# Attention and gated MLP on one core: the two output banks of a burst copied side by side into one buffer and stored with five transfers, and the loads of a stack issued in one block

## The chip, the core and the metric

The kernel runs on one NeuronCore of a Trainium2 chip. The metric is the device time of one execution in microseconds (us). A comparison is made of medians of several runs on the same chip.

## What is computed

With x of 2048 tokens by 512 features, the reference is

```python
g = sigmoid((x * gate_w).sum(-1, keepdims=True))
q, k, v = x @ wqkv                      # 32 heads of 16, sliding window of 256 keys, causal
a = softmax(mask(q k^T * 16**-0.5)) v @ wo
b = (sigmoid(x @ w_gate) * (x @ w_up)) @ w_down     # hidden width 1376
out = g * a + (1 - g) * b
```

Inputs and output are float32. The kernel splits each operand into a high and a low part and adds three products for each matmul.

## The kernel before

Tokens are handled in 16 blocks of 128 and 4 chunks of 512. The 32 heads form 8 groups of four. A *step* is one group with one chunk (32 steps), and two steps share one slot of `ring`, a buffer with three slots in which queries and keys of eight blocks stand stacked in rows: a high part, a low part, a row of zeros or ones, and a row that takes the negated maximum of each query.

The main loop (line 839) runs over *units* u, one unit per group and block, and a unit holds four heads. In unit u TensorE computes the scores of block u (`s_part`, L370), from which VectorE takes the row maxima (L376), and the transposed scores of block u - 9 (`st_part`, L425), of which ScalarE takes exponentials (L430) into `pbuf` or `pwide`. Between these matmuls stand the products of the projections (`pj`) and of the gate and up weights (`gu`), both L282. PE's order, like those of VectorE, ScalarE and SyncE (SP), is the order in which the program writes it (`manual_schedule`), and each engine works through its instructions in that order.

The maxima take a way through memory. Every fourth unit (`mark`) `max_split` (L383) makes the high and low part of the negated maxima of a step, `max_store` (L394) writes them to `max_scratch`, and `max_load` (L401, two transfers) reads them back into the ring's maximum row. `st_part` needs that row for the query blocks j to j + 2 of the same group. In units 29, 45, 61 and so on the loaded maxima are those of the third chunk of a group, and `st_part` asks for them two units later, in units 31, 47, 63. In units 21, 37 and so on they are those of the first chunk of a new group, which `st_part` asks for in the unit after the next burst.

Every eighth unit from 17 to 121 (14 units, `visits[u] == 2`) has a *burst*: `pv_part` (L460) multiplies the exponentials of two steps with v, first into the bank `pv` and then into a second bank. `o_take` (L468) copies a bank on ScalarE into a buffer `ob` (one of five buffers with the tag `sp`, which also serve the results of `gu` and `pj`) and leaves five transfers in the list `later`: four of 16 rows for the heads' outputs (`oT_d`) and one for the sums (`sum_d`). `run_dmas` (L342) issues a list on SP. In the same burst the two halves of the next stack are split (`proj_hi`, `proj_lo`) and written to `stack_scratch`.

Behind the burst, in the units with u % 8 == 2, `stack_load` (L317) makes the list `sdma` of six transfers (in the first stacks seven) that fill the next ring slot: one of constants and five from `stack_scratch`. The function `transfers` (line 859) issues what stands in `later` and then the first `SD` = 3 entries of `sdma`, so that a stack's loads are spread over two units with what is in `later` between them. The stack is used by `s_part` from the unit u % 8 == 0 that follows.

`pbuf` has 15 slots of 128 x 512. In the groups before the last the exponentials use slots 0 to 11 of it; in the last group all 15.

Of the kernel before, what the change touches and what calls it, by code (L numbers as in the profile page):

```python
# [19 lines left out]
DH = 16  # L20
HG = 4
NG = H // HG
CH = 512
NC = T // CH
# [16 lines left out]
PVLAG = LAG + 4  # L41
WIDE = 2 * 4
NWIDE = NG - 1
SD = 3
QB = 32
HOLD = 3
GAPS = [3] * 12 + [2] * 3
# [18 lines left out]
def gated_mix_kernel(  # L66
# [77 lines left out]
    with ExitStack() as actx:  # L144
# [323 lines left out]
        def o_take(s, bank):  # L468
# [5 lines left out]
                later.append((oT_d[h * DH:(h + 1) * DH, c * CH:(c + 1) * CH], ob[32 * hh:32 * hh + DH]))  # L474
            later.append((sum_d[c, g * HG:(g + 1) * HG], ob.rearrange("(h r) f -> r h f", r=32)[DH]))

        def proj(s):
            for k in range(3 * ND):
                proj_mm(s, k)
            proj_hi(s)  # L480
            proj_lo(s)
# [357 lines left out]
        for u in range(N):  # L839
            if u == LAG:  # L840
                vctx.close()
                pctx = ExitStack()
                ppool = pctx.enter_context(tc.tile_pool(name="ppool", bufs=1))
                pbuf = ppool.tile([P, 15, HG, P], F32, name="pbuf")
                pv = ps.tile([P, CH], F32, tag="pv", name="pv", bufs=1)
            if u == 1:
                proj_post(NC)
            if u == 4:
                load_gu(0, 0)
                load_gu(0, 1)  # L850
            if (u == LAG or u % 8 == 2 and u > 10) and u // 8 + 1 < NP:
                sdma = stack_load(u // 8 + 1)
            if u % 16 == 8 and u // 16 + 2 < NG:
                raw_q = load_wqk(u // 16 + 2)
            if u in (4, 8, NU):
                max_store(u // 4 - 1)
            mark = PVLAG <= u < NU and (u - PVLAG) % 4 == 0

            def transfers():
                if mark and visits.get(u) != 2:  # L860
                    run_dmas(later[:2])
                    del later[:2]
                    max_load((u - 5) // 4)
                run_dmas(later)
                later.clear()
                run_dmas(sdma[:SD])
                del sdma[:SD]

            if u in V_STORE:
                v_store(V_STORE[u])  # L870
            if not mark:
                transfers()
            if u in (5, LAG):
                max_load(u // 4 - 1)
            if u in V_LOAD:
                v_load(V_LOAD[u])
            if u in WD_LOAD:
                load_d(WD_LOAD[u])
            if u == NU:
                max_load(NSTEP - 1)  # L880
            if u in TAIL_LOAD:
                tail_load(TAIL_LOAD[u])
            if u == WO:
                both = apool.tile([P, ND, CH], F32, tag="w0", name="woraw")
                wo_raw.extend(both[:, d] for d in range(ND))
                nc.sync.dma_start(both, wo.rearrange("(c p) n -> p c n", p=P))
            for s4 in proj_at.get(u, ()):
                if u < LAG:
                    first.insert(0, (
                        lambda k, h, s4=s4: proj_slot(s4, k, h), lambda s4=s4: proj_sum(s4)))  # L890
                else:
                    work.append(proj_group(s4))
            if u == N - 1:
                hold_group(*rest.pop(0))
            for hh in range(HG):
                wide = visits.get(u) == 2
                if hh == 0 and u in visits:
                    s2 = (u - PVLAG) // 4 - wide
                    pv_part(s2, pv)
                if hh == 3 and mid(u + 1):  # L900
                    max_split((u - 4) // 4)
                if hh == 0 and mark:
                    if not mid(u):
                        max_split((u - 5) // 4)
                    run_dmas(later)
                    later.clear()
                    max_store((u - 5) // 4)
                if hh == 0 and wide:
                    flush(evac)
                    ripe = [held.pop(0) for _ in range(2) if held and held[0] // 2 == u // 8 + 1]  # L910
                    for s4 in ripe:
                        proj_hi(s4)
                    o_take(s2, pv)
                    run_dmas(later)
                    later.clear()
                    max_load((u - 5) // 4)
                    for s4 in ripe:
                        proj_lo(s4)
                    run_dmas(later)
                    later.clear()  # L920
                    second = ps.tile([P, CH], F32, tag="st", name=f"pv{s2}", bufs=2)
                    pv_part(s2 + 1, second)
                    for guests, n in ((acts, 2), (behind, 3)):
                        for _ in range(min(n, len(guests))):
                            guests.pop(0)()
                    o_take(s2 + 1, second)
                elif hh == 0 and u in visits:
                    evac.append(lambda s2=s2: o_take(s2, pv))
                if hh == 2 and mark:
                    transfers()  # L930
                if u < NU:
                    s_part(u, hh)
                if 0 <= u - LAG < NU:
                    st_part(u - LAG, hh ^ 1 if u < NU else hh)
                if u < LAG:
                    flush(behind)
                    if hh % 2 == 1:
                        upto = n_first * (2 * u + 1 + hh // 2) // (2 * LAG)
                        run_first(upto - done)
                        done = upto  # L940
                else:
                    long = u < U_WIDE
                    k8 = (u - LAG) % WIDE * HG + hh
                    dense = GAPS2[max(0, k8 - 1)] < 3 if long else u < NU and (u - PVLAG) % 4 == 3 and hh > 0
                    k = (u - PVLAG) % 4 * HG + hh
                    free = hh == 2 and not mid(u + 1) if long else k in (1, 5, 9) or k in (3, 7) and len(behind) > 2
                    if behind and (u < PVLAG or u >= NU or free):
                        behind.pop(0)()
                    if evac:
                        evac.pop(0)()  # L950
                    elif acts and not dense and (u < NU or hh % 2 == 1):
                        acts.pop(0)()
                if u >= LAG and (hh % 2 == 1 or u < NU) and (u + 1 not in visits or hh < HG - 1):
                    if u < N - 2:
                        next(slots)
            if u < LAG:
                flush(soon)
            if u == LAG - 1:
                split_gu(0, 0)
                split_gu(0, 1)  # L960
            if u in (3, 7, NU - 1):
                max_split(u // 4)
            if u // 16 + 2 < NG:
                if u % 16 == 10:
                    acts.append(lambda g=u // 16 + 2, r=raw_q: (
                        split_wqk(g, r, 0), behind.insert(0, lambda: split_wqk(g, r, 1))))
            if 0 <= u - LAG < NU:
                mask_p(u - LAG)
            if u in TAIL_SPLIT:
                acts.append(lambda d=TAIL_SPLIT[u]: tail_split(d))  # L970
            if u in WD_SPLIT:
                acts.append(lambda f=WD_SPLIT[u]: split_d(f, True))
            if u in WO_SPLIT:
                acts.extend(lambda d=d: wo_split(d) for d in range(WO_SPLIT[u], WO_SPLIT[u] + 1))
            if u in SUMS:
                sums_load(SUMS[u])
            if u - 2 in SUMS:
                behind.append(lambda c=SUMS[u - 2]: later.append(sums_invert(c)))
            if u == TREAD:
                tail_reads(0)  # L980
            if u >= TREAD:
                tail_read(0, 2)
            for n in H_LOAD.get(u, ()):
                h_load(n)
            if u == N - 1:
                pctx.close()
                lpool = actx.enter_context(tc.tile_pool(name="lpool", bufs=1))
                gates = lpool.tile([P, 4 * NB], F32, name="gates")
                gs, omg = gates[:, 0:NB], gates[:, NB:2 * NB]
                spare = [lpool.tile([P, CH], F32, name=f"spare{k}") for k in range(6)]  # L990
            if u >= N - 2:
                flush(evac)
                flush(acts)
                flush(behind)
                h_skew(u - N - 1)
# [164 lines left out]
```

## Time and profile before

| | us |
|---|---|
| median of 3 runs | 729.6 (725.34 to 729.9) |
| the profiled execution, as a run | 723.27 |
| its span, first to last instruction | 721.4 |
| PE busy | 713.5 |
| VectorE, ScalarE, GpSimd busy | 478.5, 430.4, 165.6 |
| bytes moved by DMA | 127.22 MB, 176 GB/s over the span |

The granted TensorE clock of the span is 1.000. The 14 bursts begin at 94.14, 123.88, 155.44, 184.97, 215.85, 245.22, 275.70, 305.27, 337.22, 366.59, 397.53, 426.99, 459.10 and 488.85 us: the starts of the pieces "PE pv L460" in the chain of waits. So a burst with its number of units can be found in the trace: unit 17 is at 94.14, unit 25 at 123.88, and so on in steps of eight. SPq is the queue of SyncE, whose instructions are the DMA issues; the duration of such a row is the time that the issue holds the queue, and not the time of the transfer. In a table of stretches each row gives for a stretch its length, each engine's busy time with the number of instructions, the granted clock, the mean busy share of the 16 DMA engines, and GB/s.

### The profile page before, as it was taken

How to read it: one execution, taken by the hardware profiler on the slowest of the kernel's cores; microseconds unless marked ns; L12 is line 12 of the kernel's file. 1: busy time of each engine (PE TensorE's matmuls, PEld its weight loads, DVE VectorE, ACT ScalarE, POOL GpSimd, SP SyncE). 2: the span in 40 equal slices, each digit the busy share in tenths (PEclk: the TensorE clock that was granted, in tenths of full speed). 3: DMA queues.
4: the chain of work that ended last, by engine and by line, in shares of the span. 5: the costliest groups of instructions: out<-in, count | busy, mean ns of one | idle time of the engine just before them, and what ended most of it. 6: DMA issues, size and time to landing. Idle time of an engine off the chain costs nothing.

```text
span 721.4 us, 17549 instructions
## 1 busy us (share of the span) xinstructions
PE 713.5 (99%) x6298; PEld 606.1 (84%) x6298; DVE 478.5 (66%) x1455; ACT 430.4 (60%) x890; POOL 165.6 (23%) x254
## 2 busy tenths in 40 slices
PE   9999999999999999999999999999999999999997
PEld 7888889888798798988979889798788888888886
DVE  5369767657676676765667667676837767667481
ACT  6423766667676677766767667675676655435341
POOL 5200423223233233323324223232331000000000
PEclk9999999999999999999999999999999999999999
DMA  8465534646355364554645437465478978778531
GB/s 304 112 201 195 202 123 177 189 137 212 127 195 189 121 211 146 178 165 146 203 149 197 152 99 245 151 219 148 154 216 227 263 201 215 199 169 250 144 65 58
DMA packets 104814, 127.22 MB, mean 176 GB/s; under 512 B 46718, under 2 KB 63614, under 8 KB 104728
## 3 DMA queue, kind: packets, MB, share of 16 engines
q1 hardware_dynamic: 104584, 125.98, 56.2%
q8 instruction: 49, 0.80, 0.5%
q14 instruction: 37, 0.30, 0.1%
q10 hardware_dynamic: 144, 0.13, 0.1%
HBM read 71.80 MB, written 51.13 MB: 170 GB/s over the span
## 4 chain that ended last, share of the span: by engine, by line
PE 98%; DMA 1%; issue 0%; DVE 0%; DVEq 0%
PE gu L282 28%; PE pj L282 12%; PE pv L460 11%; PE s L370 6%; PE st L425 6%; PE tp L598 6%; PE pd L96 5%; PE pd L95 5%; PE pd L94 5%; PE vh L635 3%; PE pa L94 2%; PE pa L95 2%; PE pa L96 2%; PE vps L497 2%; DMA ring<-max_scratch 1%; PE pd L1088 1%
## 5 line engine op out<-in xcount | busy, mean ns | idle before, releaser
L376 DVE CUSTOM_DVE_ANT_0 junk<-s,mask 128x384 f32<-128x384 f32 (+2 forms) x512 | 271.9, 531 | 136.8 <-PE s L370 76.4
L282 PE MATMUL gu<-xh,w 64*128 64x512 f32 x1152 | 273.5, 392 | 0.0
L282 PE MATMUL gu<-xl,w 64*128 64x512 f32 x576 | 185.9, 389 | 0.0
L430 ACT ACTIVATE pbuf<-st 128x384 f32<-128x384 f32 (+2 forms) x288 | 138.3, 490 | 60.7 <-PE st L425 31.3
L425 PE MATMUL st<-ring 64*128 64x384 f32 (+2 forms) x536 | 166.6, 327 | 2.7 <-DMA ring<-max_scratch 2.5
L370 PE MATMUL s<-ring 64*128 64x384 f32 (+2 forms) x536 | 162.9, 322 | 0.0
L282 PEld LDWEIGHTS gu<-xh,w 64*128 64x128 f32 x1152 | 157.0, 185 | 5.3
L430 ACT ACTIVATE V<-st 128x384 f32<-128x384 f32 (+2 forms) x224 | 100.6, 454 | 51.9 <-PE s L370 24.9
L370 PEld LDWEIGHTS s<-ring 64*128 64x128 f32 x536 | 95.2, 184 | 14.1 <-issue 3.0
L436 POOL TENSOR_SCALAR_AFFINE_SELECT pbuf<-pbuf 128x512 f32<-128x512 f32 x72 | 46.8, 651 | 253.2 <-ACT pbuf L430 239.1
L425 PEld LDWEIGHTS st<-ring 64*128 64x128 f32 x536 | 95.9, 184 | 7.7 <-DMA ring<-max_scratch 1.9
L282 PEld LDWEIGHTS gu<-xl,w 64*128 64x128 f32 x576 | 92.0, 185 | 1.6
L282 PE MATMUL pj<-xl,wqh 64*128 64x512 f32 (+1 forms) x228 | 79.9, 389 | 0.0
L282 PE MATMUL pj<-xh,wqh 64*128 64x512 f32 (+1 forms) x228 | 79.8, 389 | 0.0
L282 PE MATMUL pj<-xh,wql 64*128 64x512 f32 (+1 forms) x228 | 69.8, 389 | 0.0
L95 PE MATMUL pd<-ring,hb 128*128 128x512 f32 x160 | 62.3, 390 | 0.0
L94 PE MATMUL pd<-ring,hb 128*128 128x512 f32 x160 | 62.3, 390 | 0.0
L96 PE MATMUL pd<-ring,hb 128*128 128x512 f32 x160 | 62.3, 390 | 0.0
L436 POOL TENSOR_SCALAR_AFFINE_SELECT V<-V 128x512 f32<-128x512 f32 x56 | 35.8, 640 | 111.2 <-ACT V L430 107.1
L90 ACT CAST hb<-V 128x512 fp32r<-128x512 f32 x40 | 24.9, 622 | 58.8 <-DVE V L798 44.2
L460 PE MATMUL pv<-pbuf,V 128*32 128x384 f32 (+2 forms) x848 | 49.5, 382 | 0.0
L442 POOL TENSOR_SCALAR_AFFINE_SELECT pbuf<-pbuf 128x512 f32<-128x512 f32 x70 | 44.9, 641 | 0.0
(131 smaller groups left out, 1243.4 us busy)
## 6 DMA issues: line engine op xcount, KB each, us to landing
gu_scratch<-sp SPq DMA_DIRECT2D x72, 256.0 KB
V<-gu_scratch SPq DMA_DIRECT2D x36, 512.0 KB
ring<-stack_scratch SPq DMA_DIRECT2D x56, 256.0 KB
stack_scratch<-sh SPq DMA_DIRECT2D x14, 512.0 KB
stack_scratch<-sl SPq DMA_DIRECT2D x14, 512.0 KB
ring<-stack_scratch SPq DMA_DIRECT2D x14, 512.0 KB
guraw<-in_wgu_dram SPq DMA_DIRECT2D x18, 256.0 KB
v_scratch<-V SPq DMA_DIRECT2D x4, 1088.0 KB
```

Of the source, the lines that this page charges most:

```text
L94: mm(ps, lh, rh, start=first, stop=False)
L95: mm(ps, lh, rl, start=False, stop=False)
L96: mm(ps, ll, rh, start=False, stop=last)
L282: return mm(pt, (wl if w == 2 else wh)[r, d], (xl if w == 1 else xh)[r, d, c * CH:(c + 1) * CH], start=k == 0 and not second, stop=k == 3 ...
L370: mm(pt[:, (k - k0) * P:(e - k0) * P], lhsT, blk(g, k, hh, 1, e - k), start=k == k0, stop=e == i + 1, skip_group_check=True,)
L376: nc.vector.tensor_tensor_reduce(junk[:, 0:n], pt[:, 0:n], mask[:, 3 * P - n:], scale=1.0, scalar=NEG, op0=ALU.add, op1=ALU.max, accum_out ...
L425: mm(pt[:, (q - j) * P:(e - j) * P], lhsT, blk(g, q, hh, 0, e - q), start=q == j, stop=e == last, skip_group_check=True,)
L430: exps.append(nc.scalar.activation(p_blk(u, hh, 0, n), pt[:, 0:n * P].rearrange("p (b t) -> p b t", t=P), AF.Exp, scale=SCALE,))
L436: nc.gpsimd.affine_select(buf[:, s0], buf[:, s0], pattern=[[0, HG], [1, P]], compare_op=ALU.is_ge, fill=0.0, base=0, channel_multiplier=-1,)
L442: nc.gpsimd.affine_select(old, old, pattern=[[0, HG], [-1, P]], compare_op=ALU.is_gt, fill=0.0, base=0, channel_multiplier=1,)
L460: mm(bank[32 * hh:32 * hh + w, (q - q0) * P:(e - q0) * P], vt[:, v:v + w], p_blk(g * NB + j, hh, q - j, e - q), start=j == j0, stop=j == q ...
L598: return mm(tp[b][:, 0:TW], (xl if w == 1 else xh)[r, d, b * P:(b + 1) * P], tw[d][int(w == 2)][r, 0:TW], start=k == 0 and not second, sto ...
```

## The change

The first copy of a burst goes to slot 12 of `pbuf`, the second to slot 13 (`o_copy`). Nothing is stored after the first one. After the second, `o_store` leaves five transfers for both: four of 16 rows of 1024 (two chunks, which lie side by side in `oT_d`), one for the sums of two chunks. The `run_dmas(later)` after the first copy is gone. `SD` is 7 after unit 13, so that all entries of `sdma` go in the first unit behind the burst. `o_take` stays for the units that take one step at a time (after unit 121).

```diff
-SD = 3
+SD = 7
...
+        def o_copy(half, bank):
+            nc.scalar.copy(pbuf[:, 12 + half].rearrange("p h t -> p (h t)"), bank)
+
+        def o_store(s):
+            g, c = divmod(s, NC)
+            both = pbuf[:, 12:14].rearrange("p s h t -> p (s h t)")
+            for hh in range(HG):
+                h = g * HG + hh
+                later.append((oT_d[h * DH:(h + 1) * DH, c * CH:(c + 2) * CH], both[32 * hh:32 * hh + DH]))
+            later.append((
+                sum_d[c:c + 2, g * HG:(g + 1) * HG].rearrange("c h f -> h c f"),
+                both.rearrange("(h r) (c f) -> r h c f", r=32, c=2)[DH],
+            ))
...
-                run_dmas(sdma[:SD])
-                del sdma[:SD]
+                n = SD if u > PVLAG else 3
+                run_dmas(sdma[:n])
+                del sdma[:n]
...
-                    o_take(s2, pv)
-                    run_dmas(later)
-                    later.clear()
+                    o_copy(0, pv)
                     max_load((u - 5) // 4)
...
-                    o_take(s2 + 1, second)
+                    o_copy(1, second)
+                    o_store(s2)
```

PE, VectorE, ScalarE and GpSimd carry out the same instructions in the same order before and now; of ScalarE's, 28 copies write `pbuf` instead of `ob`. Only SP's queue is shorter, by 70 transfers, and in another order. Its rows in the burst of unit 25 (at 123.88 us), with a number of equal transfers at the end of a row, before:

```order
L394 DMA max_scratch<-nt_1883 128x32
L344 DMA oT_scratch<-ob_1890 16x512 x4
L344 DMA sum_scratch<-ob_1890 4x512
L401 DMA ring<-max_scratch 4x16x32 x2
L344 DMA stack_scratch<-sh_1886 128x1024
L344 DMA stack_scratch<-sl_1887 128x1024
L344 DMA oT_scratch<-ob_1928 16x512 x4
L344 DMA sum_scratch<-ob_1928 4x512
```

SP's rows at the same place now:

```order
L394 DMA max_scratch<-nt_1876 128x32
L401 DMA ring<-max_scratch 4x16x32 x2
L344 DMA stack_scratch<-sh_1879 128x1024
L344 DMA stack_scratch<-sl_1880 128x1024
L344 DMA oT_scratch<-pbuf 16x1024 x4
L344 DMA sum_scratch<-pbuf 4x2x512
```

The load of the maxima follows their store directly, and five transfers are gone from ahead of everything behind it. SP's rows after that, in units 25 to 29 (the loads of the stack and the next round of maxima), before:

```order
L533 DMA guraw_0_1973<-in_wgu_dram 128x512
L344 DMA gu_scratch<-sp_0_0_1971 128x512
L344 DMA ring<-fill_scratch 4x2x1024
L344 DMA ring<-stack_scratch 32x4x1024
L344 DMA ring<-stack_scratch 32x2x1024
L344 DMA gu_scratch<-sp_1_0_2008 128x512
L344 DMA gu_scratch<-sp_2_0_2037 128x512
L344 DMA ring<-stack_scratch 32x2x1024 x3
L394 DMA max_scratch<-nt_2162 128x32
L401 DMA ring<-max_scratch 4x16x32 x2
```

SP's rows in those units now:

```order
L547 DMA guraw_0_1959<-in_wgu_dram 128x512
L344 DMA gu_scratch<-sp_0_0_1957 128x512
L344 DMA ring<-fill_scratch 4x2x1024
L344 DMA ring<-stack_scratch 32x4x1024
L344 DMA ring<-stack_scratch 32x2x1024 x4
L344 DMA gu_scratch<-sp_1_0_1997 128x512
L344 DMA gu_scratch<-sp_2_0_2026 128x512
L394 DMA max_scratch<-nt_2148 128x32
L401 DMA ring<-max_scratch 4x16x32 x2
```

The last three loads of the stack have moved ahead of two stores of `gu` results. In the bursts of units 33, 57, 81 and 105 no such store stood between the loads, and they went in one block before as well; after the burst of unit 121 no stack is left to load. So nine of the 14 bursts have their loads moved.

## The prediction

> **What bounds the kernel now.** I read the busy shares first, then the chain that ended last, then the span cut at the bursts, and only then SP's queue. The first two say the same: TensorE has work nearly all the time.
>
> ```profile
> PE 713.5 (99%) x6298; PEld 606.1 (84%) x6298; DVE 478.5 (66%) x1455; ACT 430.4 (60%) x890; POOL 165.6 (23%) x254
> PE 98%; DMA 1%; issue 0%; DVE 0%; DVEq 0%
> ```
>
> The change takes nothing from PE. It can only give back time in which PE stands, and that is at most 721.4 - 713.5 = 7.9 us of idle time in the whole span, plus what hides in slow stretches inside "busy". To find it I cut the span from the start of one burst to the start of the next. Of the 13 stretches these are the six that begin with a burst for the third and fourth chunk of a group (units 25, 41, 57, 73, 89, 105), which hold the same work but for one thing named below:
>
> ```profile
> 123.88:155.44 31.56, 31.19 (x344) 27.30 (x348) 20.76 (x77) 21.06 (x45) 9.20 (x15) 1.00 0.52 166
> 184.97:215.85 30.88, 30.77 (x333) 26.75 (x336) 20.71 (x76) 20.72 (x44) 9.19 (x15) 1.00 0.49 167
> 245.22:275.70 30.48, 30.48 (x333) 26.56 (x336) 21.50 (x78) 22.09 (x47) 9.18 (x15) 1.00 0.52 178
> 305.27:337.22 31.95, 31.19 (x345) 27.62 (x348) 20.75 (x77) 21.11 (x45) 9.19 (x15) 1.00 0.47 155
> 366.59:397.53 30.94, 30.79 (x333) 26.62 (x336) 21.15 (x77) 20.69 (x44) 9.46 (x15) 1.00 0.49 168
> 426.99:459.10 32.11, 30.76 (x328) 27.30 (x328) 20.50 (x77) 21.59 (x46) 9.19 (x15) 1.00 0.55 184
> ```
>
> Their lengths differ by up to 1.63 us at a full clock (1.00). Over the shortest, 30.48, they have 1.08, 0.40, 0, 1.47, 0.46 and 1.63: 5.04 us together. Two of them (units 25 and 73) hold some 12 matmuls more, where a window of blocks crosses the end of the ring. What such pieces cost is seen in four of the other stretches, which differ in nothing else:
>
> ```profile
> 94.14:123.88 29.74, 29.74 (x321) 26.15 (x324) 20.84 (x73) 20.06 (x44) 9.64 (x15) 1.00 0.48 165
> 155.44:184.97 29.53, 29.53 (x314) 24.03 (x313) 19.68 (x72) 20.54 (x45) 9.19 (x15) 1.00 0.53 174
> 215.85:245.22 29.37, 29.37 (x313) 24.27 (x313) 20.12 (x72) 19.94 (x44) 9.64 (x15) 1.00 0.49 167
> 275.70:305.27 29.57, 29.57 (x320) 26.20 (x324) 20.14 (x72) 19.48 (x43) 9.64 (x15) 1.00 0.53 165
> ```
>
> Eight more make (29.74 + 29.57)/2 - (29.53 + 29.37)/2 = 0.21 us, so twelve about 0.31, twice 0.62. That leaves 5.04 - 0.62 = 4.4 us of standing in the first kind of stretch, and nothing to speak of in the second. The waits say on what:
>
> ```profile
> PE st L425 <- DMA ring<-max_scratch: 2.5, 3, 1.4
> SPq L401 <- DMA max_scratch<-nt: 55.5, 16, 5.0
> ```
>
> PE waits for the maxima that come back from memory, and SP, before it may load them, waits up to 5.0 us for their store to land. Why so long is seen in SP's queue in the stretch of unit 25 (start, time that the issue holds the queue), and in the share of the DMA engines at the same time:
>
> ```profile
> 125.44 0.32 SPq L394 DMA_DIRECT2D max_scratch<-nt  x1
> 127.28 1.71 SPq L344 DMA_DIRECT2D oT_scratch<-ob  x4
> 129.04 0.55 SPq L344 DMA_DIRECT2D sum_scratch<-ob  x1
> 129.69 1.14 SPq L401 DMA_DIRECT2D ring<-max_scratch  x2
> 130.88 0.45 SPq L344 DMA_DIRECT2D stack_scratch<-sh  x1
> ...
> 132.96 2.09 SPq L344 DMA_DIRECT2D oT_scratch<-ob  x4
> ...
> 137.28 1.27 SPq L344 DMA_DIRECT2D ring<-stack_scratch  x2
> 138.66 0.99 SPq L344 DMA_DIRECT2D gu_scratch<-sp  x2
> 139.71 2.05 SPq L344 DMA_DIRECT2D ring<-stack_scratch  x3
> 142.41 0.33 SPq L394 DMA_DIRECT2D max_scratch<-nt  x1
> 147.64 1.16 SPq L401 DMA_DIRECT2D ring<-max_scratch  x2
> ```
>
> ```profile
> 130.00:132.00 2.00, 2.00 (x25) 1.91 (x22) 1.34 (x6) 1.25 (x4) 0.00 (x0) 1.00 0.18 53
> 136.00:138.00 2.00, 2.00 (x22) 1.69 (x21) 1.48 (x6) 1.58 (x4) 1.22 (x2) 1.00 0.37 119
> 142.00:144.00 2.00, 2.00 (x22) 2.00 (x20) 1.63 (x7) 1.58 (x4) 1.22 (x2) 1.00 0.97 377
> 144.00:146.00 2.00, 2.00 (x22) 2.00 (x20) 1.41 (x6) 1.66 (x5) 0.00 (x0) 1.00 0.94 364
> 146.00:148.00 2.00, 2.00 (x23) 2.00 (x21) 1.22 (x7) 1.95 (x6) 1.23 (x2) 1.00 0.09 27
> ```
>
> From 127 to 142 us SP issues without a break while the engines are partly idle (0.18, 0.37); then they are full (0.97, 0.94), and the small store of 142.41 comes through only when that queue is empty, at about 147.6. So the loads of the stack start late because SP is late, and the store of the maxima stands behind them. The load of 147.64 lands 1.9 us later, and PE has by then stood. The counterexample is the shortest stretch:
>
> ```profile
> 257.99 3.19 SPq L344 DMA_DIRECT2D ring<-stack_scratch  x5
> 264.39 0.34 SPq L344 DMA_DIRECT2D gu_scratch<-sp  x1
> 264.82 0.62 SPq L394 DMA_DIRECT2D max_scratch<-nt  x1
> 266.88 1.19 SPq L401 DMA_DIRECT2D ring<-max_scratch  x2
> ```
>
> Here the five loads went in one block 6.8 us ahead of the store, SP had caught up, and the maxima could be loaded 266.88 - 264.82 = 2.06 us after the store was issued.
>
> **The change part by part.** *Five transfers fewer.* The first four and the sums hold SP from 127.28 to 129.59, 2.3 us. Without them the load of the maxima follows its store after 2.06 us at the best, at 127.5 instead of 129.69: 2.2 us earlier. The merged stores must wait for the second copy, which is done here at 129.26 + 0.59 = 129.85 (row below), against a start at 132.96; so the gain stays between 2.2 and 3.1 us. I take 2.2.
>
> ```profile
> 129.26 0.59 ACT L471 COPY ob<-pv 128x512 f32<-128x512 f32 x1 [2.00 <-DMA oT_scratch<-ob]
> ACT ob L471 <- DMA oT_scratch<-ob: 4.0, 2, 2.0
> ```
>
> *The copies.* ScalarE makes as many, of the same size (0.59 us). It no longer waits for a buffer of the five, which cost at most 4.0 us in two places; but here the second product ended just before the copy began, so I count nothing. Slots 12 and 13 are free but for the stores of the burst before, issued some 25 us earlier: no wait.
>
> *The stores.* They carry the same bytes in rows twice as long. Nobody reads `oT_d` or `sum_d` until the last units, so a slower landing costs nothing. That the first bank is stored 3 us later costs nothing for the same reason.
>
> *The block of loads.* Three loads move ahead of two `gu` stores, which hold SP 0.99 us. All of them stand ahead of the maxima's store either way, so it gains nothing by that; the stack itself is not waited for before or now. Behind the block the `gu` stores go 2.05 us later than without it, and 2.2 earlier by the part above. If a late store held a `gu` buffer, ScalarE and then PE's bank would wait. The stretch of unit 33 had the block before and is 29.53 against 29.37: at most 0.16 us in each of the nine bursts that are changed, 1.4 us; at least nothing. I take nothing, since the 2.2 us cover it; without that cover it is the 1.4.
>
> *The sum.* In the long stretches the store of the maxima finds a queue that began 2.2 us earlier, so its wait falls from 5.2 (142.41 to 147.64) to about 3, and the load is that much earlier. The longest standing is 1.63 us, so all five vanish: -4.4 us. If the queue's end moves by less, say by half (1.1), 4.4 shrinks to what lies under 1.1 in each (1.08 - 0.31, 0.40, 1.1, 0.46, 1.1) = 3.8. What is late next is nothing in these stretches: with the wait gone they are as the one of unit 57, in which PE is busy 30.48 of 30.48. The profiled execution goes from 723.27 to 718.9. That execution is 6.3 us under the median of the runs; from the median, 729.6 - 4.4 = 725.2.
>
> The Trainium skill (DMA: Bandwidth & Descriptors, "Issuing engines are not separate DMA queues") speaks against this: starting a transfer is "usually small relative to the DMA itself", and all transfers end on the same 16 engines. By that rule SP's 2.3 us would be worth nothing, the sum 0 and the time 729.6. The rows of 130 and 136 us disagree: with SP at work without a break, the engines were at 0.18 and 0.37.
>
> **The rivals.** *The bytes bound it.* From 142 to 146 us the engines are full; if what follows the burst is set by when data are ready (the stack must be written before it is read back, 130.88 to 137.28) and by 16 engines, an earlier SP changes nothing and the store lands as late as now: 729.6. For it speak 0.97 and 0.94, against it 0.37 at 136, just as the loads begin. The rule of the Trainium skill named above would end here.
>
> *The block delays the maxima.* The stretch of unit 105 already had its loads in one block, and it is the longest:
>
> ```profile
> 439.71 3.19 SPq L344 DMA_DIRECT2D ring<-stack_scratch  x5
> 446.82 0.32 SPq L394 DMA_DIRECT2D max_scratch<-nt  x1
> 451.41 1.19 SPq L401 DMA_DIRECT2D ring<-max_scratch  x2
> ```
>
> If a deeper queue is what holds the store, all six become like it: 6 x 1.63 - 5.04 = +4.7 us, 734.3. It decides against me if the wait from the maxima's store to their load (4.59 here) does not fall. Against it: unit 57 has the block and waits 2.06; what unit 105 has more are loads of weights behind the block.
>
> *The runs hold more of the same waits.* The median is 6.3 us over the profiled execution. If that is more standing at the same place and goes as well: 729.6 - 4.4 - 6.3 = 718.9. Nothing in one profile shows it; the spread of the runs (725.34 to 729.9) allows it.
>
> **How the numbers follow.** The forecast has 0.62, the bytes 0.15, the block 0.10, more of the same waits 0.13. The likeliest time is 725.2, its own range 721.7 to 727.2: at the low end all of PE's 7.9 us of idle time, at the high end half the shift with the late `gu` stores, -3.8 + 1.4. The range takes in 718.5 and, for the bytes, 731.5 with the scatter of the runs; the block's 734.3 is left out. A measurement of this kernel can tell about 1% from no change, 7.3 us. Faster than 722.3 are the third rival and the forecast's edge: 0.18. Slower than 736.9 is only the block's case with more on top: 0.06. The rest, 0.76, is within 1%.
>
> **What would show it.** In the profile after, in the stretches of units 25 to 105: the first load of maxima about 2.1 us after its store and SP's later rows 2 to 3 us earlier; from the second store of maxima to its load about 3 us or less in place of 5.2; no row in which PE waits for `max_scratch`; the five long stretches at 30.5 to 30.8. The stretches of 29.4 to 29.7 stay. I am wrong if the second load of maxima is as late as now, or if the stretches stay long without that wait, or if ScalarE's copies of `gu` begin to wait for stores.

## The result and the profile after

The changed kernel takes 718.83 us (median of 4 runs, 718.68 to 720.11), the kernel before 728.95 us beside it (4 runs, 725.34 to 729.9). The ratio is 0.9888, with a 95% interval from 0.9846 to 0.993: 1.1% faster. On another chip, with more runs of before, it was 719.69 against 724.77, ratio 0.9918 (0.9895 to 0.9942). The profiled execution of the changed kernel took 718.91 us, that of before 723.27: 4.4 us apart, which is what the sum had said.

The six stretches from a burst for the third and fourth chunk to the next one, after:

```profile
124.15:155.04 30.89, 30.89 (x345) 26.89 (x348) 20.75 (x77) 21.06 (x45) 9.19 (x15) 1.00 0.56 169
184.55:214.93 30.38, 30.38 (x333) 26.03 (x331) 20.68 (x76) 20.69 (x44) 9.19 (x15) 1.00 0.52 170
244.34:274.83 30.49, 30.49 (x333) 26.69 (x336) 21.51 (x78) 22.07 (x47) 9.18 (x15) 1.00 0.53 179
304.41:335.20 30.79, 30.79 (x344) 27.10 (x348) 20.74 (x77) 21.05 (x45) 9.19 (x15) 1.00 0.50 161
364.52:395.25 30.73, 30.73 (x333) 26.25 (x336) 21.13 (x77) 20.75 (x44) 9.45 (x15) 1.00 0.51 171
424.64:455.05 30.41, 30.41 (x330) 24.54 (x329) 20.61 (x77) 21.48 (x46) 9.19 (x15) 1.00 0.60 194
```

PE is busy for the whole length of each. Together they take 183.69 us against 187.92, 4.2 less; the other seven take 206.60 against 206.79, and the head and the tail of the span differ by 0.3 and 0.1. No row of PE's waits names `max_scratch` any more. SP's queue in the stretch of unit 25, which begins at 124.15 (before at 123.88):

```profile
125.71 0.32 SPq L394 DMA_DIRECT2D max_scratch<-nt  x1
127.16 1.13 SPq L401 DMA_DIRECT2D ring<-max_scratch  x2
128.34 0.45 SPq L344 DMA_DIRECT2D stack_scratch<-sh  x1
...
130.15 2.48 SPq L344 DMA_DIRECT2D oT_scratch<-pbuf  x4
...
134.89 3.19 SPq L344 DMA_DIRECT2D ring<-stack_scratch  x5
138.18 1.25 SPq L344 DMA_DIRECT2D gu_scratch<-sp  x2
142.69 0.32 SPq L394 DMA_DIRECT2D max_scratch<-nt  x1
145.19 1.19 SPq L401 DMA_DIRECT2D ring<-max_scratch  x2
```

Counted from the start of the burst, the loads of the stack begin at 10.7 us (before 13.4) and their last ones are through SP at 13.9 (before 17.9). The second store of maxima is issued at the same point, 18.5, but waits 2.5 us for its end and no longer 5.2. SP is idle ahead of it for 3.3 us (139.43 to 142.69); before, it had caught up only 0.65 us ahead of the store. The DMA engines show the same, in two of the rows that the prediction shows for before:

```profile
136.00:138.00 2.00, 2.00 (x23) 1.73 (x21) 1.50 (x5) 1.58 (x5) 1.22 (x2) 1.00 0.89 188
...
144.00:146.00 2.00, 2.00 (x21) 2.00 (x20) 1.38 (x5) 1.53 (x4) 0.24 (x1) 1.00 0.06 14
```

Their share at 136 was 0.37 and is 0.89; at 144 it was 0.94 and is 0.06. The stack's bytes have moved earlier.

### The profile page after: what moved, and what is told of

It reads as the page before. It is cut to its first block, busy times and chain, and to the rows that moved or that the text cites. A ratio compares the mean times of both kernels' runs of the same rounds, so it can differ in the third digit from the quotient of the medians.

```text
span 717.2 us, 17422 instructions
## 1 busy us (share of the span) xinstructions
PE 711.9 (99%) x6298; PEld 599.9 (84%) x6298; DVE 478.3 (67%) x1455; ACT 430.3 (60%) x890; POOL 165.6 (23%) x254
## 4 chain that ended last, share of the span: by engine, by line
PE 98%; DMA 1%; SPq 0%; ACT 0%; issue 0%; DVE 0%; DVEq 0%
PE gu L282 28%; PE pj L282 12%; PE pv L460 11%; PE s L370 6%; PE st L425 6%; PE tp L612 6%; PE pd L96 5%; PE pd L94 5%; PE pd L95 5%; PE vh L649 3%; PE pa L94 2%; PE pa L95 2%; PE pa L96 2%; PE vps L511 1%; DMA V<-in_xT_dram 1%; PE pd L1101 1%
## 5 line engine op out<-in xcount | busy, mean ns | idle before, releaser
L282 PE MATMUL gu<-xl,w 64*128 64x512 f32 x576 | 183.4, 389 | 0.0
L282 PEld LDWEIGHTS gu<-xh,w 64*128 64x128 f32 x1152 | 153.2, 184 | 7.5
L282 PEld LDWEIGHTS gu<-xl,w 64*128 64x128 f32 x576 | 89.6, 184 | 2.1
```

The lines of the kernel that those rows point to most:

```text
L282: return mm(pt, (wl if w == 2 else wh)[r, d], (xl if w == 1 else xh)[r, d, c * CH:(c + 1) * CH], start=k == 0 and not second, stop=k == 3 ...
```

## The experiments

Five readings were to be told apart. *Late queue* (mine): SP is late behind a burst by the issue of five transfers, so the stack's loads end late, the store of the maxima lands late and PE stands. *Block*: the gain comes from the loads ahead of the `gu` stores. *Buffers*: it comes from ScalarE no longer waiting for one of five. *Early maxima*: what counts is the burst's own load of maxima. *Bytes*: what the removed transfers cost is work of the DMA engines. Besides, the median of before stood 6 us over its profiled execution, and that wanted an explanation: more standing at the same place (*same waits*), or time lost in another part of the span (*elsewhere*).

The results in one table. "Six" is the sum of the six stretches of the kernel's own profile, "idle" PE's waits for `max_scratch` there. A ratio below 1 is faster than before; it is worked out from the single runs and can differ a little from the quotient of the medians.

| kernel | median us | of before, same chip | ratio (95% interval) | six, us | idle, us |
|---|---|---|---|---|---|
| before again | 725.49 | 726.19 | 1.0005 (0.9988 to 1.0023) | 189.29 | 4.0 |
| stores only | 720.48 | 726.19 | 0.9933 (0.9909 to 0.9956) | 183.65 | 0 |
| block only | 727.32 | 726.19 | 1.0019 (0.9996 to 1.0042) | 189.46 | 4.3 |
| changed, first five stores again | 725.86 | 726.19 | 0.9999 (0.9983 to 1.0015) | 188.27 | 3.4 |
| before, first stores moved back | 725.01 | 724.77 | 0.9997 (0.9973 to 1.0021) | 188.78 | 3.4 |
| before, two loads a unit | 725.92 | 724.77 | 1.0004 (0.9981 to 1.0027) | 191.41 | 4.6 |
| before, maxima by GpSimd | 740.12 | 724.77 | 1.0198 (1.0164 to 1.0231) | 199.94 | 11.7 |
| changed again | 719.69 | 724.77 | 0.9918 (0.9895 to 0.9942) | 184.46 | 0.4 |
| changed, five tiny transfers | 728.17 | 725.73 | 1.0022 (1.0 to 1.0045) | 187.48 | 2.2 |
| changed, stores parked | 726.07 | 725.73 | 0.9995 (0.9971 to 1.002) | 184.76 | 0 |
| before, third profile | 728.81 (one run) | | | 192.77 | 6.1 |
| before, fourth profile | 723.7 (one run) | | | 188.20 | 3.1 |

### The stores and the block apart

Stores only is the changed kernel with

```diff
-SD = 7
+SD = 3
```

> The merged stores without the block of loads (SD = 3). Late queue (SP is late behind the burst by five transfers): all or nearly all of the gain, 718.5 to 720.5 us, no wait of PE on max_scratch. Block (the gain comes from the loads ahead of the gu stores): as before, 727 to 730.

Block only is the kernel before with `SD = 7` behind unit 13 and `o_take` as it was.

> The block of loads with the ten stores of before. Late queue: the last three loads are issued about 1 us earlier and the rest as late as before, so part of the standing stays, 722 to 728 us. Block: all of the gain, 719 us. Block delays the maxima (my second rival): slower than before, 731 or more.

The stores alone bring it: 0.7% faster, no wait, the six stretches as in the changed kernel. The block alone brings nothing, by its interval. Together they are at 0.9918 (the changed kernel again), and that interval overlaps the one of the stores alone; the block's share cannot be told from zero.

> The changed kernel once more, beside the kernel before on this chip. Late queue: 7 us or so faster than before here, as the stores-only kernel was 5.7 faster; the block adds 0 to 1 us to that. Block: the block adds 2 us or more to what the stores give.

The block alone shows a wait that I had not expected, in the stretch of unit 113, which is 31.48 us long against 29.75. PE's waits, SP's queue and ScalarE there:

```profile
PE st L425 <- ACT V L430: 1.4, 1, 1.4
```

```profile
473.51 3.18 SPq L344 DMA_DIRECT2D ring<-stack_scratch  x5
476.73 0.58 SPq L575 DMA_DIRECT2D tailraw<-in_wgu_tail_dram  x1
```

```profile
482.02 0.57 ACT L588 CAST tail_hb<-tailraw 128x450 fp32r<-128x450 f32 x1 [2.24 <-DMA tailraw<-in_wgu_tail_dram]
```

The load of a tail weight stood ahead of the last three loads before (472.38), and stands behind all five now. ScalarE waits 2.24 us for it, and PE 1.4 us for ScalarE. In the changed kernel the queue is earlier and the stretch is 29.70 us long: the five transfers fewer pay for the block. Where they were put back, below, the stretch is long again (30.99 and 30.59).

### Is it the transfers, their issue time or the buffers?

The changed kernel, with the first bank also stored by itself, as before:

```diff
                     o_copy(0, pv)
+                    one = pbuf[:, 12].rearrange("p h t -> p (h t)")
+                    for k5 in range(HG):
+                        h5 = g5 * HG + k5
+                        later.append((oT_d[h5 * DH:(h5 + 1) * DH, c5 * CH:(c5 + 1) * CH], one[32 * k5:32 * k5 + DH]))
+                    later.append((sum_d[c5, g5 * HG:(g5 + 1) * HG], one.rearrange("(h r) f -> r h f", r=32)[DH]))
+                    run_dmas(later)
+                    later.clear()
                     max_load((u - 5) // 4)
```

> The changed kernel, whose first bank is also stored by itself right behind its copy, with the five transfers of before (the same bytes are stored again later): SP's queue is that of the block-only kernel, while the copies go to pbuf and no buffer of the five is used. Late queue: as the block-only kernel within 1.5 us, 722 to 728. Buffers (the gain comes from ScalarE no longer waiting for one of the five): as the changed kernel, 719.

Five transfers more, with the copies in `pbuf`, take the whole gain away (0.9999). So the buffers had no part in it. Next, five transfers of next to no bytes in the same place:

```diff
                     max_load((u - 5) // 4)
+                    for k5 in range(5):
+                        nc.sync.dma_start(pad_d[k5], mask[0:16, 16 * k5:16 * k5 + 16])
```

> The changed kernel with five further transfers of 16 rows of 64 bytes (a constant into a scratch that nobody reads) between the burst's load of maxima and the stores of the stack: SP is held as long as by the five stores that the change removed, the DMA engines get next to no bytes. Late queue by issue time: the stack's loads are 2 us later again and the time is back near that of the kernel before, within 2 us. Bytes (what the removed stores cost was their work on the DMA engines): as the changed kernel, 719 to 720.

It is the issue time. SP's queue in the stretch of unit 25 of this kernel:

```profile
128.00 2.31 SPq L932 DMA_DIRECT2D pad_scratch<-mask  x5
...
137.32 3.19 SPq L345 DMA_DIRECT2D ring<-stack_scratch  x5
140.61 1.08 SPq L345 DMA_DIRECT2D gu_scratch<-sp  x2
142.34 0.32 SPq L395 DMA_DIRECT2D max_scratch<-nt  x1
147.71 1.19 SPq L402 DMA_DIRECT2D ring<-max_scratch  x2
```

Five transfers of 1 KB hold SP 2.31 us, as much as the five removed ones of 136 KB (2.3), the loads of the stack begin 13.5 us from the start of the burst as they did before (13.4), and the load of the maxima follows their store after 5.4 us again. The median is that of before, if anything 0.2% over it.

### The place of the first stores

```diff
                     o_take(s2, pv)
-                    run_dmas(later)
-                    later.clear()
                     max_load((u - 5) // 4)
```

> The kernel before, whose first five stores are only issued behind the burst's load of maxima: ten stores still stand ahead of the loads of the stack. Late queue: SP reaches the loads of the stack as late as before, so the time is that of before within 1.5 us, with the same wait of PE. Early maxima (what counts is that the burst's own load of maxima comes 2 us earlier): the gain of the changed kernel, 5 to 7 us.

Ratio 0.9997: in the stretch of unit 25 the burst's load of maxima comes 2.8 us earlier from the start of the burst (3.0 against 5.8), and that is worth nothing as long as ten stores stand ahead of the stack's loads.

### A smaller block

The kernel before with `n = 2` for u over 13.

> The kernel before with two loads of a stack in each of three units (SD = 2), so that two go one unit later. Late queue: the end of the loads moves nearer to the second store of maxima or past it, the six stretches grow by up to 1 us each, 0 to 6 us slower. Bytes (the queue is full anyway and its order does not matter): as before within 1 us.

The median does not move (1.0004). Its profile has a long six (191.41), in which one stretch alone has 34.83 us; the section on the hardware shows why. But the loads end only 0.3 us later on SP's queue (18.2 us from the start of the burst in unit 25, against 17.9): SP has not caught up by then, and going a unit later in the program is hardly later on the queue. So the delay that was to be tried was not given, and this run does not tell the two readings apart.

### The maxima on GpSimd's queue

`max_store` and `max_load` with `nc.gpsimd.dma_start`.

> The kernel before with the store and the loads of the maxima issued on GpSimd's queue; SP keeps its ten stores and is as late as before. Late queue (the maxima's store stands behind the stack's loads in one queue): it lands early although SP is late, PE does not wait for max_scratch, 718 to 722 us. Bytes (the 16 engines are full, whoever issues): the store still lands when the stack's loads end, 725 to 728. If GpSimd itself is late for the issue, behind its own work, PE waits at the same place for that, 728 or more.

2.0% slower (1.6 to 2.3%), and my expectation of 718 to 722 us missed. The store is now on a queue of its own, and the profile has for a transfer issued by GpSimd the time to its landing. GpSimd's rows in the stretch of unit 25, the landing of that store, the shortest, median and longest landing of all stores and loads of maxima, and the share of the DMA engines meanwhile:

```profile
144.81 0.60 POOL L394 DMA_DIRECT2D max_scratch<-nt  x1 [2.64 <-ACT pr L295]
...
150.08 1.28 POOL L401 DMA_DIRECT2D ring<-max_scratch  x2 [3.42 <-PE gu L282]
```

```profile
max_scratch<-nt POOLq DMA_DIRECT2D x1, 16.0 KB, 4.6
DMA to landing us min/median/max: 1.7/2.6/6.4
```

```profile
144.00:146.00 2.00, 2.00 (x21) 1.96 (x20) 1.68 (x7) 1.73 (x5) 1.18 (x2) 1.00 1.06 418
146.00:148.00 2.00, 2.00 (x22) 2.00 (x20) 1.40 (x6) 1.67 (x5) 0.66 (x2) 1.00 0.52 192
```

Counted from the start of the burst (125.55 here) the store is issued only 0.7 us later than SP's was. It lands 4.6 us after that, at 149.4, and the load is issued 0.6 us later: the 3.42 us that GpSimd stands ahead of the load end with the landing, and not with GpSimd's own work, although the row names PE. The loads of the stack were issued on SP's queue, from 138.6 to 143.5, and filled the engines (1.06, then 0.52). So a queue of its own does not get the small store through beside them; that they share the engines is enough to hold it. Whether its place in SP's queue adds to that in the kernel before is not shown. Then the two loads of maxima land late as well, 3.8 us after their issue in the median (1.9 in the stretch before the change), beside a load of v that SP now issues ahead of them, at 148.66 and no longer behind them; PE stands 3.4 us. Of the expectation's three cases the mechanism of the second came (the store lands when the stack's loads end), at a higher price than its 725 to 728 us.

### The stores out of the way altogether

The changed kernel with the five merged stores issued in the units with u % 8 == 6:

```diff
-                later.append((oT_d[...], both[32 * hh:32 * hh + DH]))
+                parked.append((oT_d[...], both[32 * hh:32 * hh + DH]))
...
+            if u % 8 == 6 and parked:
+                later.extend(parked)
+                parked.clear()
```

> The changed kernel with the five merged stores issued only five units behind the burst, past the second load of maxima. Late queue: the stack's loads start 2 to 3 us earlier still; where the changed kernel waits no more it gains nothing, where it still stood (0.4 to 0.8 us in the stretch of unit 105) that goes: 718 to 720, 0 to 1 us under the changed kernel. Against it: the stores now stand ahead of the load of v and of the next gu stores; if these are waited for, slower than the changed kernel.

The gain is gone (0.9995), but PE never waits for the maxima. Most of it is lost at one place behind unit 121:

```profile
513.35 1.82 SPq L344 DMA_DIRECT2D oT_scratch<-pbuf  x4
515.21 0.55 SPq L344 DMA_DIRECT2D sum_scratch<-pbuf  x1
```

```profile
517.24 0.49 ACT L430 ACTIVATE pbuf<-st 128x384 f32<-128x384 f32 x1 [4.79 <-DMA sum_scratch<-pbuf]
```

In the last group the exponentials use slots 12 and 13, and they wait 4.8 us until the parked stores have read them. PE stands 3.26 us for that and then has half its clock for a while (0.71 and 0.50 in the rows of 518 and 520 us; see the section on the hardware). From the last burst to the end it takes 238.01 us against 232.45. In the changed kernel these stores are issued at 490.75, long before the slots are needed. A second loss is in the stretch of unit 105 (31.64 us against 30.41), as the expectation had allowed for:

```profile
PE pv L460 <- DMA V<-v_scratch: 1.2, 1, 1.2
```

The load of v stands behind the parked stores there and is issued 25.8 us from the start of the burst instead of 23.5. Without these 1.2 us the six stretches are as in the changed kernel (184.76 and 183.69), so there was nothing to win in the bursts.

### The other executions of the kernel before

> The kernel before, unchanged, profiled once more; its runs took 725.3 to 729.9 us where the profiled execution took 723.3. Same waits (my third rival): if this profile is of an execution near 728, the six stretches that begin at the bursts of units 25 to 105 hold about 5 us more than the 187.9 us of the first profile, and PE waits longer on max_scratch. Elsewhere: these stretches stay at 187.9 and the extra time lies ahead of unit 17, behind unit 121, or in the other seven stretches.

> The kernel before, profiled a third time, to see an execution of another length. Same waits: its length differs from the first profile's 721.4 us span by as much as the six stretches of units 25 to 105 differ from 187.9 us, within 0.5 us (but for what the head ahead of unit 17 differs). Elsewhere: the difference lies in the rest of the span.

> As the run before: one more execution of the kernel before; the difference of its span from 721.4 us is that of the six stretches from 187.9 us within 0.5 us, or else lies elsewhere.

Spans of 721.4, 722.7, 726.1 and 722.0 us have six of 187.92, 189.29, 192.77 and 188.20: span less six is 533.5, 533.4, 533.3 and 533.8. The executions differ in those six stretches and almost nowhere else, so it is the same waits (in the third, with what follows one of them: a stretch of 35.29 us, see the section on the hardware). The runs of the last three profiles took 724.39, 728.81 and 723.7 us.

## Why the prediction was right, and where its size was not

*The bound and the place.* Right. The standing was in the six stretches, 4.4 us by the sum and 4.2 by the profile after. The five long ones came down to 30.38 to 30.89 us, about the 30.5 to 30.8 that were forecast.

*Five transfers fewer.* Right, and sized from below. The burst's load of maxima follows its store after 1.45 us (127.16 less 125.71), not 2.06, and the merged stores begin 3.1 us earlier from the burst's start, the upper end of my 2.2 to 3.1. That the price is SP's issue and not bytes is shown by the tiny transfers. I had set the Trainium skill against it (DMA: Bandwidth & Descriptors, "Issuing engines are not separate DMA queues"). Its first half agrees with the traces: that transfers end on the same 16 engines, whoever issues them, fits the store of the maxima issued by GpSimd (4.6 us to its landing beside the stack's loads, 1.7 at the best). What did not come true is the conclusion of nothing that I had drawn from its second half, that starting a transfer is usually small beside the transfer: five starts of 0.46 us add up to 2.31, and putting them back takes the whole gain away.

*Why the second store lands late.* Right that the loads of the stack hold it and that they are late because SP is late. That it "stands behind them" and comes through when "that queue is empty" is shown for the engines only: on a queue of its own, beside the same loads, it still took 4.6 us to land.

*The copies and the block at nothing.* Both shown: with the ten transfers back, the copies in `pbuf` and the block win nothing. My bound for the block, 1.4 us by late `gu` stores in nine bursts, was near by luck: without the cover it costs 1.7 us in one stretch (unit 113, 31.48 against 29.75), by the load of a tail weight.

*The sum.* From one profile to the other it is -4.4, as forecast. From median to median it is -10.1 (by the ratio 1.1%, or 8.2). The 718.83 us lie 6.4 under the forecast of 725.2 and below its own range (721.7 to 727.2), close to the lower end, 718.5, that the whole range had with the rivals. Two terms were off. The first is the base: 729.6 was a median of three runs, while 87 other runs of before, on three chips, have a median of 725.6, and only 6 of them reach the 728.95 of the result. Why the first runs were so long is not known. From 725.6 the same -4.4 gives 721.2. The second is the standing itself, which makes up the 1.5 to 2.4 us from there to the 719.69 and 718.83 measured: I took it from one execution that was among the shortest. Of the four profiles of before, the six stretches lie 4.2, 5.6, 9.1 and 4.5 us over those of the changed kernel. This was the third rival, to which I gave 0.13, and the spread of the runs (725.34 to 729.9) had spoken for it. That its 718.9 was met to 0.1 us is luck: it took all of the 6.3 us between the median and the profile for standing, and where the changed kernel ran again, beside 23 runs of before, the gain is 5.1 us (5.9 by the ratio).

*The other rivals.* That the bytes of the removed stores bound it is refuted by the tiny transfers; that full engines keep the store of the maxima from landing is right, and SP's lateness decides when they are full. That the block delays the maxima is not borne out. What was special in unit 105 is not settled: there the load of the maxima follows their store after 2.71 us in the first profile of the changed kernel (4.59 before), but after 3.75 in the second, in which PE still stands 0.4 us.

## What to carry to other kernels

Where one queue issues everything, count its issues between a result and the transfer that somebody waits for: 0.32 to 0.64 us each in the rows shown here (up to 1.0 in the kernel with the first stores moved back, where four took 4.02), and as long for 1 KB as for 32. Merging stores that nobody is in a hurry for can pay through the loads behind them. Look for the slack of such a wait before spreading transfers out or moving them back: the same stores, moved five units on, were waited for by a buffer's next user, and held up a load that PE waited for. And where runs of a kernel spread by more than its rivals do, take the size of a wait from several executions.

## What the runs showed of the hardware

I had not expected that a wait of PE costs more than its length. In the third profile of before PE stands 2.54 us in the stretch of unit 25, and soon after has half its clock for 3.4 us; the third-last figure of a row is the granted clock, here a mean over 2 us, and in the last row over just those 3.4:

```profile
151.66 0.32 PE L425 MATMUL st<-ring 64*128 64x128 f32 x1 [2.54 <-DMA ring<-max_scratch]
```

```profile
150.00:152.00 2.00, 0.34 (x3) 0.34 (x5) 0.25 (x2) 0.00 (x0) 0.37 (x1) 1.00 0.15 46
152.00:154.00 2.00, 2.00 (x14) 1.96 (x13) 0.56 (x2) 0.98 (x2) 0.00 (x0) 0.55 1.02 250
154.00:156.00 2.00, 2.00 (x16) 1.98 (x14) 0.57 (x3) 0.49 (x1) 0.00 (x0) 0.60 0.64 250
156.00:158.00 2.00, 2.00 (x24) 2.00 (x23) 1.12 (x6) 1.27 (x3) 1.09 (x2) 1.00 0.02 7
```

```profile
152.20:155.60 3.40, 3.40 (x22) 3.34 (x20) 1.13 (x4) 1.30 (x3) 0.00 (x0) 0.50 0.89 261
```

That stretch is 35.29 - 30.89 = 4.4 us over the one of the changed kernel, and only 2.5 of it is standing. Half a clock for 3.4 us is worth 1.7 us, an estimate that makes up most of the rest. In the kernel with two loads a unit, 2.45 us of idle time are followed by a clock of 0.71 and 0.50:

```profile
455.48 0.41 PE L425 MATMUL st<-ring 64*128 64x384 f32 x1 [2.45 <-DMA ring<-max_scratch]
```

```profile
456.00:458.00 2.00, 2.00 (x17) 2.00 (x15) 0.61 (x3) 1.78 (x4) 0.00 (x0) 0.71 0.91 358
458.00:460.00 2.00, 2.00 (x12) 2.00 (x12) 1.23 (x4) 1.10 (x3) 0.00 (x0) 0.50 0.39 144
```

After 1.71 us, in the kernel that stores the first bank again, the clock stays whole:

```profile
453.85 0.41 PE L425 MATMUL st<-ring 64*128 64x384 f32 x1 [1.71 <-DMA ring<-max_scratch]
```

```profile
454.00:456.00 2.00, 2.00 (x20) 2.00 (x22) 0.68 (x3) 1.71 (x4) 0.00 (x0) 1.00 0.91 264
```

The nearest pair is in the kernel with the maxima by GpSimd, where the clock stays whole after 1.93 us and falls after 2.41:

```profile
344.27 0.32 PE L425 MATMUL st<-ring 64*128 64x128 f32 x1 [1.93 <-DMA ring<-max_scratch]
539.30 0.42 PE L460 MATMUL pv<-pbuf,V 128*32 128x128 f32 x8 [2.41 <-POOL pbuf L436]
```

```profile
344.00:346.00 2.00, 1.73 (x16) 1.72 (x18) 0.45 (x1) 0.90 (x2) 1.42 (x3) 1.00 0.00 0
346.00:348.00 2.00, 2.00 (x24) 1.93 (x23) 1.25 (x6) 1.07 (x3) 0.06 (x1) 1.00 0.00 0
540.00:542.00 2.00, 2.00 (x18) 1.85 (x16) 0.35 (x1) 1.36 (x3) 0.00 (x0) 0.72 0.04 8
542.00:544.00 2.00, 2.00 (x14) 1.76 (x14) 0.34 (x2) 0.87 (x2) 0.98 (x2) 0.50 0.30 66
```

So in these traces a second price of about 2 us sets in somewhere between 1.93 and 2.41 us of idle time. The Trainium skill (TensorE: Matmul & The Clock Gate, Part 1, The HAM clock gate) has the clock halve after an idle window of about 3.4 us; here less idle time than that was enough, as far as the modelled ends of matmuls show it.

The kernel before stands near that edge: in its four profiles PE stands up to 1.4, 1.4, 2.5 and 1.1 us at a time. Of the 87 runs on three chips, 56 have a mean clock of 0.999 or 1 and a median of 724.6 us, and 31 have 0.998 or less and a median of 727.4 (up to 732.0). The 10 runs of the changed kernel all have 0.999 or 1 and lie between 718.7 and 720.2. The spread is thus a part of what the change took away; that the longest runs of before hold such a drop is seen in one profile, and for the others it is argued from the mean clock.
